# Mean squares of the attended tokens from small fp32 matmuls, and values of the key stage on other partitions

## The chip, the cores and the metric

One core of a Trainium2 chip runs the whole program. The metric is the device time of one execution in microseconds (us); the median of three runs stands for the kernel.

## The reference

Attention through a small set of packed tokens, followed by two feed-forward blocks. With 8 batches, 8 heads, 576 tokens of 64 numbers a head and 32 packed tokens a head:

```python
p_packed = sm_attn(p, k, v)                  # 32 packed tokens a head look at the keys
out = sm_attn(q, p_packed, p_packed)         # 576 tokens a head look at the 32 packed ones
x = out.transpose(0, 2, 1, 3).reshape(4608, 512)
xn = x / sqrt(mean(x * x, axis=-1) + 1e-06) * rms_g
x = (silu(xn @ w_gate) * (xn @ w_val)) @ w_out      # 512 -> 1536 -> 512
h = x @ w2_in                                        # 512 -> 2048
return (h * cos(h)) @ w2_out                         # 2048 -> 512
```

`sm_attn` is softmax attention with the maximum subtracted. All results are fp32; the weights arrive as 64-bit floats.

## The kernel before, in words

The program goes through three stages.

The **key stage** works on 16 groups, each four heads of a batch, in a loop of 18 rounds that handles several groups at different steps (lines 613 to 663). For a group it transposes the keys (`kp`), multiplies them with the packed tokens (`s`), takes the exponential (`e`), transposes it in 96-column chunks (`et`, copied to `eT`) and multiplies it with the values (`pp`, from the tile `vn`). The values of a group lie on 96 partitions, three blocks `m` of 32, each loaded by a DMA of its own (`load_v`, lines 345 to 352). The result `cd`, 32 packed outputs of four heads by 64 numbers, is stored to DRAM (`c`) and read again later. Beside this the loop narrows weights from 64 to 32 bits (`wy`, `ny`) and attends for batch 0.

The **projection stage** (lines 844 to 902) makes 24 iterations for each batch: in each, `gv_block` does 12 matmuls of 288 columns into two PSUM banks (gate and value), ScalarE and VectorE turn them into `silu` and `shl`, and `acc_block` does 6 matmuls of 512 columns of an earlier iteration into `acc`. Between them the attention of the next batch, `attend(b + 1)`, is fed in: it is a generator, and `att_step` advances it at two points of every iteration, by as many steps as its plan is due. All results of attention steps go through the pool of four banks that gate and value use (`ps_gv`); in the key stage, batch 0 uses a pool of two (`ps_bg`). `unit` makes a projection weight for a batch with 64x32 matmuls (`mps`).

The **last stage** does the second feed-forward block (`hp`, `ops`) and takes about half of the span.

In `attend`, softmax is done with 96 tokens on the partitions (tile `s`), in two halves `hf` of 288 tokens. The attended token itself is never formed: the weight `unit` makes is already multiplied with the packed outputs. Only its mean square is needed, so that `s` can be scaled by its inverse root. The steps are named in a string, two characters of which are the half and a part:

```python
    ATT_ORD = "t00 t01 x00 x01 x02 x03 t10 r00 t11 s00 x10 x11 p00 x12 p01 x13 - r10 - s10 - p10 p11"
```

Step `t` transposes the softmax of four heads into 128 rows (`atp`) and splits it into a high and a low part (`ahl`). Step `x` multiplies it with a block-diagonal matrix of packed outputs (`bdf`, split into `bdh`) by three matmuls (high by high, high by low, low by high: `mm3`), which gives two heads' 128 columns, squares the result on ScalarE and adds it into `ssq` on VectorE. Step `r` sums over the partitions with a matmul against ones (`rp`) and raises to the power -0.5 on GpSimd; `s` scales the softmax, `p` transposes it again for the projections (`apt`). A dash is a step that does nothing. The list for batch 0 is `ATT_ORD0`; its first `ATT_U` steps are done in the key stage's loop, the rest just behind it.

All instructions up to the middle of the last stage stand on each engine in the order in which the code issues them (`tc.manual_schedule()`); every DMA is issued by SyncE's queue.

Of the kernel before, what the change touches and what calls it, by code (L numbers as in the profile page):

```python
# [20 lines left out]
def kernel(  # L21
# [40 lines left out]
    REST = S - 512  # L62
    R_LOAD, R_SPLIT, S_AT = (1, 2), (4, 5), (20, 21, 24 + 1, 24 + 2)
# [3 lines left out]
    ATT_U, U_ATT = 34, 5  # L67
# [94 lines left out]
    nc.gpsimd.memset(ones, 1.0)  # L162
# [27 lines left out]
    bdf = a1.tile([128, 2, 4, D], F32, name="bdf")  # L190
    mhalf = a1.tile([CP, CH], F32, name="mhalf")
    for t in (bq, bdf):
        nc.gpsimd.memset(t, 0.0)
# [17 lines left out]
    def att_load(b):  # L211
        for r in range(2):
            rows = slice(r * 64, (r + 1) * 64)
            nc.sync.dma_start(out=bq[rows, :, r * NP:(r + 1) * NP], in_=q_dram[b][rows])
        for h in range(4):
            rows = slice(h * NP, (h + 1) * NP)
            nc.sync.dma_start(out=bdf[rows, :, h, :], in_=c_dram[b][rows])

    def attend(b):
# [28 lines left out]
        bdh = a1.tile([128, 2, 2, 4 * D], F32R, tag="bdh", name="bdh")  # L248
        hilo(bdf.rearrange("p g h d -> p g (h d)"), bdh[:, 0], bdh[:, 1])
# [18 lines left out]
        def transposed(dst, hf, kt):  # L268
# [6 lines left out]
            hilo(tp, dst[:, 0, kt], dst[:, 1, kt])  # L275

        z = [{}, {}]
# [6 lines left out]
        def a_x(hf, j):  # L284
            ahl = z[hf]["ahl"]
            if j == 0:
                z[hf]["acc"] = a1.tile([128, HALF], F32, tag="ssq", name="ssq")
            acc = z[hf]["acc"]
            g, r = divmod(j, 2)
            xp = psb[0].tile([128, HALF], F32, tag="mm", name="xp")  # L290
            mm3(
                xp, bdh[:, 0, g, r * 128:(r + 1) * 128], bdh[:, 1, g, r * 128:(r + 1) * 128],
                ahl[:, 0, g], ahl[:, 1, g], True, True,
            )
            if j == 0:
                nc.scalar.activation(out=acc, in_=xp, func=AF.Square)
            else:
                sq = a1.tile([128, HALF], F32, tag="sq", name="sq")
                nc.scalar.activation(out=sq, in_=xp, func=AF.Square)
                nc.vector.tensor_tensor(out=acc, in0=acc, in1=sq, op=ALU.add)  # L300

        def a_r(hf, _):
            acc = z[hf]["acc"]
            rp = psb[0].tile([CP, CH], F32, tag="mm", name="rp")
            for c in range(CH):
                nc.tensor.matmul(rp[:, c:c + 1], acc[:, c * CP:(c + 1) * CP], ones[:, 0:1], start=True, stop=True)
            ri = z[hf]["ri"] = a2.tile([CP, 2, CH], F32, tag="ri", name="ri")
            nc.vector.tensor_scalar(
                out=ri[:, 0], in0=rp, scalar1=1.0 / DM, scalar2=1e-6, op0=ALU.mult, op1=ALU.add
# [3 lines left out]
        def a_s(hf, _):  # L313
            ri = z[hf]["ri"]
            for c in range(CH):
                cc = hf * CH + c
                nc.vector.tensor_scalar(
                    out=s[:, cc], in0=s[:, cc], scalar1=ri[:, 1, c:c + 1], scalar2=None, op0=ALU.mult
                )

        def a_p(hf, kt):
            if kt == 0:
                ap_t[b, hf] = a3p[0].tile([128, 2, 2, HALF], F32R, tag="apt", name="apt")
            transposed(ap_t[b, hf], hf, kt)
# [288 lines left out]
    for i in range(NG + 2):  # L613
# [10 lines left out]
        if i == U_ATT:  # L624
            att_load(0)
# [420 lines left out]
```

## Time and profile before

| | |
|---|---|
| median of 3 runs (lowest to highest) | 1711.57 us (1710.38 to 1719.77) |
| profiled execution | 1720.5 us, of which the span of its instructions is 1718.7 |
| TensorE matmuls busy | 1657.4 us, 96% of the span |
| TensorE weight loads busy | 1378.2 us, 80% |
| VectorE (DVE) busy | 1009.4 us, 59% |
| ScalarE (ACT) busy | 848.7 us, 49% |
| GpSimd (POOL) busy | 78.3 us, 5% |
| mean granted clock of TensorE | 0.984 |

PE is TensorE's matmuls, PEld its weight loads, SP SyncE. Matmuls are pipelined: one begins before the one before it has ended, so the cost of a matmul in a dense stretch is the distance from its start to the next start, not its duration. An fp32 matmul of the program appears as two matmuls in the trace, one of fp32r (the split parts) as one; a transpose is one. A wait is put down to the instruction that came last by the profile; where the one named had long been done, it was another, often a DMA.

### The profile page before, as it was taken

Reading aid. Unit: us, or ns where it says so; the run is one execution under the profiler, and the core shown is the slowest. Engines: PE = TensorE matmul, PEld = TensorE weight load, DVE = VectorE, ACT = ScalarE, POOL = GpSimd, SP = SyncE. Lnnn points to the kernel's source line nnn. Section 1 sums busy time; section 2 is a strip of 40 time slices with the busy share of each in tenths; the row PEclk is TensorE's granted clock in tenths of the full one; section 3 lists DMA queues with packets and bytes.
Section 4 is the critical chain, followed back from the end, with each engine's and each line's share of the span. In section 5 each row is a group of like instructions: output and inputs, shape, how many; then the busy total and the mean of one; then the engine's idle time right before and its main releaser. Section 6 shows DMA issues by size and latency. Waiting matters only on the chain.

```text
span 1718.7 us, 26344 instructions
## 1 busy us (share of the span) xinstructions
PE 1657.4 (96%) x10176; PEld 1378.2 (80%) x10176; DVE 1009.4 (59%) x1958; ACT 848.7 (49%) x1595; POOL 78.3 (5%) x81
## 2 busy tenths in 40 slices
PE   6777989999999999999999999999999999999998
PEld 4555778888888888888888888888888888888887
DVE  2567875656565656665343675656555556565554
ACT  3454555545454545454433554545454545554453
POOL 0000431000000000000011000000000000000000
PEclk9887999999999999999999999999999999999999
DMA  9996745454545545543246010100000000000001
GB/s 203 247 284 172 223 147 162 138 171 142 177 128 167 154 139 163 166 139 108 77 135 256 25 54 21 34 16 28 22 25 25 25 25 25 25 0 25 1 25 25
DMA packets 112285, 177.36 MB, mean 103 GB/s; under 512 B 50208, under 2 KB 64544, under 8 KB 112160
## 3 DMA queue, kind: packets, MB, share of 16 engines
q1 hardware_dynamic: 112160, 175.68, 34.6%
q8 instruction: 80, 1.31, 0.3%
q14 instruction: 45, 0.37, 0.1%
HBM read 134.22 MB, written 41.42 MB: 102 GB/s over the span
## 4 chain that ended last, share of the span: by engine, by line
PE 84%; DMA 0%; DVE 0%; SPq 0%; issue 0%
PE hp L159 8%; PE hp L157 8%; PE hp L158 8%; PE ops L159 8%; PE ops L157 8%; PE ops L158 8%; PE gv L157 6%; PE acc L157 5%; PE gv L158 5%; PE gv L159 5%; PE acc L159 5%; PE acc L158 5%; PE mps L558 2%; PE sp L237 1%; PE atp L271 1%; PE qtp L227 1%
## 5 line engine op out<-in xcount | busy, mean ns | idle before, releaser
L157 PE MATMUL gv<-apt,wmhl 128*128 128x288 f32 x768 | 236.9, 308 | 2.4 <-DVE ahl L106 1.4
L158 PE MATMUL gv<-apt,wmhl 128*128 128x288 f32 x768 | 227.0, 296 | 0.0
L159 PE MATMUL gv<-apt,wmhl 128*128 128x288 f32 x768 | 226.7, 295 | 0.0
L158 PE MATMUL hp<-xhl,wmhl 128*128 128x512 f32 x576 | 224.1, 389 | 0.0
L159 PE MATMUL hp<-xhl,wmhl 128*128 128x512 f32 x576 | 224.1, 389 | 0.0
L157 PE MATMUL ops<-w2hl,ghl 128*128 128x512 f32 x576 | 224.1, 389 | 0.0
L158 PE MATMUL ops<-w2hl,ghl 128*128 128x512 f32 x576 | 224.1, 389 | 0.0
L157 PE MATMUL hp<-xhl,wmhl 128*128 128x512 f32 x576 | 223.9, 389 | 0.0
L159 PE MATMUL ops<-w2hl,ghl 128*128 128x512 f32 x576 | 222.3, 389 | 0.0
L946 ACT ACTIVATE r<-r 128x512 f32<-128x512 f32 x144 | 91.0, 632 | 250.0 <-DVE r L945 250.0
L954 DVE TENSOR_TENSOR r<-r,hp 128x512 f32<-128x512 f32 x144 | 98.8, 686 | 164.8 <-ACT r L947 164.7
L157 PEld LDWEIGHTS gv<-apt,wmhl 128*128 128x128 f32 x768 | 144.9, 189 | 44.5 <-issue 10.2
L157 PE MATMUL acc<-shl,wohl 128*128 128x512 f32 x432 | 175.8, 407 | 0.4 <-DMA shl<-s 0.4
L158 PE MATMUL acc<-shl,wohl 128*128 128x512 f32 x432 | 169.9, 393 | 2.8 <-DVE shl L753 2.8
L159 PE MATMUL acc<-shl,wohl 128*128 128x512 f32 x432 | 170.4, 394 | 0.0
L941 ACT ACTIVATE kk<-hp,magic 128x512 f32<-128x512 f32 x144 | 99.1, 688 | 117.4 <-PE hp L159 117.2
L742 DVE TENSOR_TENSOR silu<-silu,gv 128x288 f32<-128x288 f32 x192 | 86.5, 450 | 113.3 <-PE gv L159 96.7
L749 ACT ACTIVATE shl<-silu 128x288 fp32r<-128x288 f32 x192 | 85.1, 443 | 132.4 <-DVE silu L742 131.4
L158 PEld LDWEIGHTS gv<-apt,wmhl 128*128 128x128 f32 x768 | 145.1, 189 | 3.2
L159 PEld LDWEIGHTS gv<-apt,wmhl 128*128 128x128 f32 x768 | 144.6, 188 | 0.0
L942 DVE TENSOR_SCALAR kk<-kk 128x512 f32<-128x512 f32 x144 | 61.4, 426 | 116.2 <-ACT kk L941 116.1
L159 PEld LDWEIGHTS hp<-xhl,wmhl 128*128 128x128 f32 x576 | 108.2, 188 | 22.6
(126 smaller groups left out, 2857.6 us busy)
## 6 DMA issues: line engine op xcount, KB each, us to landing
wy<-wy SPq DMA_DIRECT2D x96, 512.0 KB, 4.4
kn<-in_k_dram SPq DMA_DIRECT2D x16, 576.0 KB, 7.7
vn<-in_v_dram SPq DMA_DIRECT2D x48, 192.0 KB, 6.6
qnat<-in_q_dram SPq DMA_DIRECT2D x32, 288.0 KB, 4.8
x_dram<-x SPq DMA_DIRECT2D x18, 512.0 KB, 3.2
x1raw<-x_dram SPq DMA_DIRECT2D x18, 512.0 KB, 4.0
raw<-in_moe_w_in_dram SPq DMA_DIRECT2D x16, 512.0 KB, 4.3
raw<-in_moe_w_out_dram SPq DMA_DIRECT2D x16, 512.0 KB, 4.2
```

The lines of the kernel that those rows point to most:

```text
L157: nc.tensor.matmul(ps, lhi, rhi, start=first, stop=False)
L158: nc.tensor.matmul(ps, lhi, rlo, start=False, stop=False)
L159: nc.tensor.matmul(ps, llo, rhi, start=False, stop=last)
L227: nc.tensor.transpose(tp[:, c * CP:(c + 1) * CP], qv[:, i, 2 * c:2 * c + 2, :].rearrange("p c d -> p (c d)"), ident[:CP, :CP],)
L237: nc.tensor.matmul(sp[:, i, 2 * c:2 * c + 2, :], qT[:, i, c * CP:(c + 1) * CP], bq[:, 2 * j + i], start=True, stop=True,)
L558: nc.tensor.matmul(ps[kt][h * NP:(h + 1) * NP], ppT[b // 4][rows, 4 * kt + h, n:n + NP], w_y[2 * u + kt][rows, j], start=True, stop=True,)
L742: nc.vector.tensor_tensor(out=t, in0=t, in1=pss[1], op=ALU.mult)
L749: nc.scalar.activation(out=sh[:, 0, cols], in_=t, func=AF.Copy)
L941: nc.scalar.activation(out=kk, in_=hp, func=AF.Identity, scale=1.0 / TWO_PI, bias=magic[:, 0:1])
L942: nc.vector.tensor_scalar(out=kk, in0=kk, scalar1=-MAGIC, scalar2=None, op0=ALU.add)
L946: nc.scalar.activation(out=r, in_=r, func=AF.Abs)
L954: nc.vector.tensor_tensor(out=r, in0=r, in1=hp, op=ALU.mult)
```

## The change

The mean squares are computed with unsplit fp32 operands, a head at a time. Step `t` only copies the transposed softmax (`at`, all four pieces of a batch in one tile). The packed outputs are loaded as they are stored (`cl`, one DMA a batch at its own place), not into a block-diagonal tile, and aren't split. Step `x` now takes a group `kt` of four heads: for each half and head one matmul of 32 rows (the head's packed tokens) and 64 columns (its numbers), the first half to PSUM partitions 0 to 63, the second to 64 to 127, each head in a bank of its own. So the four banks hold all tokens of the four heads. They are squared and summed as before, and one `r` step does both halves: `ones` has a column for the upper and one for the lower 64 partitions. There are two `x` steps a batch (for batch 0, whose pool has two banks, two heads at a time). An `x` step beside the projections runs between the two halves of an `acc_block` (the argument `mid`); the attention's plan has 38 steps in place of 45, and the key stage's loop does 29 steps of batch 0 in place of 34.

In the key stage, values lie on partitions 16 to 111 of a 128-partition tile whose other rows are zero; the blocks are loaded in the order 0, 2, 1. The exponential gets 16 zero columns at either end, and is transposed in pieces of 128 columns that begin 16 ahead of each chunk, so that rows and values meet. Three fixed value tiles take the place of a rotating buffer of three, and `cd` has two buffers in place of three.

```diff
+    V_P = 16
-    ATT_U, U_ATT = 34, 5
+    ATT_U, U_ATT = 29, 5
...
-    ATT_ORD = "t00 t01 x00 x01 x02 x03 t10 r00 t11 s00 x10 x11 p00 x12 p01 x13 - r10 - s10 - p10 p11"
-    ATT_ORD0 = "t00 t01 x00 x01 x02 x03 r00 s00 t10 t11 x10 x11 x12 x13 r10 s10 p00 p01 p10 p11"
-    AL_AT = 16
-    ATT_FROM, ATT_TO, ATT_FROM0, N_ATT = 0, 48, 10, 45
+    ATT_ORD = "t00 t10 - x00 t01 t11 - x10 - - r00 - s00 p00 p01 s10 p10 p11"
+    ATT_ORD0 = "t00 t10 x00 x01 t01 t11 x10 x11 - r00 - s00 s10 p00 p01 p10 p11"
+    AL_AT, CL_AT = 16, 21
+    ATT_FROM, ATT_TO, ATT_FROM0, N_ATT = 0, 48, 10, 38
...
-    nc.gpsimd.memset(ones, 1.0)
+    nc.gpsimd.memset(ones, 0.0)
+    for r in range(2):
+        nc.gpsimd.memset(ones[r * 64:(r + 1) * 64, r:r + 1], 1.0)
...
-        for h in range(4):
-            rows = slice(h * NP, (h + 1) * NP)
-            nc.sync.dma_start(out=bdf[rows, :, h, :], in_=c_dram[b][rows])
+
+    def att_load_c(b):
+        nc.sync.dma_start(out=cl, in_=c_dram[b])
...
-        bdh = a1.tile([128, 2, 2, 4 * D], F32R, tag="bdh", name="bdh")
-        hilo(bdf.rearrange("p g h d -> p g (h d)"), bdh[:, 0], bdh[:, 1])
...
         def a_t(hf, kt):
-            if kt == 0:
-                z[hf]["ahl"] = a1.tile([128, 2, 2, HALF], F32R, tag="ahl", name="ahl")
-            transposed(z[hf]["ahl"], hf, kt)
+            if (hf, kt) == (0, 0):
+                z["at"] = a1.tile([128, 2, 2, HALF], F32, tag="at", name="at")
+            nc.scalar.activation(out=z["at"][:, kt, hf], in_=transposed(hf, kt), func=AF.Copy)
...
+        def a_x(kt, part):
+            at = z["at"]
+            hs = range(4) if b else range(2 * part, 2 * part + 2)
+            xp = {h: psb[0].tile([128, HALF], F32, tag="mm", name="xp") for h in hs}
+            for hf in range(2):
+                for h in hs:
+                    rows = slice(h * NP, (h + 1) * NP)
+                    nc.tensor.matmul(
+                        xp[h][hf * 64:(hf + 1) * 64], cl[rows, kt, :], at[rows, kt, hf], start=True, stop=True
+                    )
+            for h in hs:
+                if (kt, h) == (0, 0):
+                    z["acc"] = a1.tile([128, HALF], F32, tag="ssq", name="ssq")
+                    nc.scalar.activation(out=z["acc"], in_=xp[h], func=AF.Square)
+                else:
+                    sq = a2.tile([128, HALF], F32, tag="sq", name="sq")
+                    nc.scalar.activation(out=sq, in_=xp[h], func=AF.Square)
+                    nc.vector.tensor_tensor(out=z["acc"], in0=z["acc"], in1=sq, op=ALU.add)
...
+    v_t = [u2.tile([128, 4, NC_, D], F32, tag=f"vn{x}", name="vn", bufs=1) for x in range(3)]
+    for x in range(2):
+        nc.vector.memset(v_t[x], 0.0)
+    e_pad = u2.tile([128, 2 * V_P + S], F32, tag="e", name="e", bufs=1)
+    for x in (slice(0, V_P), slice(V_P + S, 2 * V_P + S)):
+        nc.vector.memset(e_pad[:, x], 0.0)
...
-        for m in range(CH):
-            nc.sync.dma_start(out=vn[m * 32:(m + 1) * 32], in_=vs[m])
+        for m in (0, 2, 1):
+            nc.sync.dma_start(out=vn[V_P + m * 32:V_P + (m + 1) * 32], in_=vs[m])
...
-                nc.tensor.transpose(et[:, c, :], e[:, cc * CP:(cc + 1) * CP], ident)
+                nc.tensor.transpose(et[:, c, :], e_pad[:, cc * CP:cc * CP + 128], ident)
...
-    def acc_block(n, f, d2):
+    def acc_block(n, f, d2, mid=None):
...
         for r in range(2):
+            if r and mid:
+                mid()
...
-        while att is not None and att_done[0] < want:
+        while att is not None and att_done[0] < want and mid == (att_next[0] == "x"):
             att_done[0] += 1
-            next(att, None)
+            att_next[0] = next(att, None) or ""
...
-            acc_block(*seq[i - LAG])
+            acc_block(*seq[i - LAG], mid=(lambda: att_step(2 * i + 1, True)) if i < len(seq) else None)
```

The first place in the order is TensorE in a late batch of the projection stage, while batch 2 attends: an `x` step that stands ahead of a unit (`mps`), in the kernel before. `xp` is what the squares are taken of, a bracket names the engines (or DMA semaphores) that a row waits for.

```order
L157 MATMUL acc<-shl,wohl 128x512
L158 MATMUL acc<-shl,wohl 128x512
L159 MATMUL acc<-shl,wohl 128x512
L157 MATMUL xp<-ahl,bdh 128x288 [waits DVE_49]
L158 MATMUL xp<-ahl,bdh 128x288
L159 MATMUL xp<-ahl,bdh 128x288
L558 MATMUL mps<-wy,ppT_173 32x512 [waits DMAHW6_49,Activation_49]
L558 MATMUL mps<-wy,ppT_173 32x512 [waits DMAHW7_49,DVE_49]
L558 MATMUL mps<-wy,ppT_173 32x512 x6
```

After the change the same engine has this there: the first half of an acc block has just ended.

```order
L291 MATMUL xp<-at,cl 64x288 [waits DMAHW4_49,Activation_49]
L291 MATMUL xp<-at,cl 64x288 [waits DVE_49]
L291 MATMUL xp<-at,cl 64x288 [waits Activation_49]
L291 MATMUL xp<-at,cl 64x288 [waits DVE_49]
L291 MATMUL xp<-at,cl 64x288 x4
L158 MATMUL acc<-shl,wohl 128x512
L159 MATMUL acc<-shl,wohl 128x512
L160 MATMUL acc<-shl,wohl 128x512
L271 MATMUL atp<-ident,s 128x96 [waits Activation_49]
L271 MATMUL atp<-ident,s 128x96 x2
L566 MATMUL mps<-wy,ppT_175 32x512 [waits DMAHW5_49,Activation_49]
L566 MATMUL mps<-wy,ppT_175 32x512 [waits DMAHW6_49,Activation_49]
```

The `x` step has gone from the end of the acc block into its middle, waits for four banks one after the other, and the unit's matmuls behind it wait for ScalarE.

The second place is TensorE at the end of the key stage, from the last group's transposed exponentials to the first gate matmul, in the kernel before.

```order
L424 MATMUL et<-ident,e 96x128 x6
L452 MATMUL tp<-ident,cd 128x128
L157 MATMUL xp<-ahl,bdh 128x288
L158 MATMUL xp<-ahl,bdh 128x288
L159 MATMUL xp<-ahl,bdh 128x288
L438 MATMUL pp<-vn,eT 32x64 x24
L306 MATMUL rp<-ones,ssq 96x1 x3
L452 MATMUL tp<-ident,cd 128x128
L271 MATMUL atp<-ident,s 128x96 x12
L157 MATMUL gv_2116<-apt,wmhl 128x288
```

After the change:

```order
L432 MATMUL et<-ident,e 128x128 x6
L460 MATMUL tp<-ident,cd 128x128
L446 MATMUL pp<-vn,eT 32x64 x24
L460 MATMUL tp<-ident,cd 128x128
L271 MATMUL atp<-ident,s 128x96 x12
L158 MATMUL gv_2066<-apt,wmhl 128x288
```

The `x` and `r` steps of batch 0 no longer stand among the last groups' matmuls; they have moved to earlier rounds of the loop.

## Rows read from the trace of the kernel before

**Rows 1.** The page's busy times: us, share of the span, instructions.

```profile
PE 1657.4 (96%) x10176; PEld 1378.2 (80%) x10176; DVE 1009.4 (59%) x1958; ACT 848.7 (49%) x1595; POOL 78.3 (5%) x81
```

**Rows 2.** Windows: stretch, length, busy us (instructions) by engine, clock, DMA share, GB/s.

```profile
0.00:50.00 50.00, 32.94 (x360) 23.64 (x361) 12.91 (x39) 17.76 (x42) 3.94 (x20) 0.90 0.97 201
50.00:100.00 50.00, 40.57 (x495) 29.98 (x495) 27.98 (x69) 24.80 (x60) 1.62 (x6) 0.86 0.99 262
100.00:166.70 66.70, 45.47 (x626) 31.24 (x623) 47.70 (x120) 34.14 (x82) 3.21 (x5) 0.79 0.84 230
166.70:300.00 133.30, 124.79 (x900) 104.13 (x899) 95.30 (x191) 69.78 (x152) 39.77 (x26) 0.99 0.57 174
300.00:850.00 550.00, 550.00 (x3929) 471.35 (x3928) 329.33 (x732) 275.57 (x583) 14.08 (x12) 1.00 0.46 145
```

**Rows 3.** Timeline, PE, 29 to 49 us: start, us, instruction [idle before, releaser].

```profile
32.56 0.70 PE L381 MATMUL kp<-ident,kn 128*128 128x128 f32 x3 [3.01 <-ACT eT L425]
...
35.87 1.51 PE L438 MATMUL pp<-vn,eT 96*32 96x64 f32 x48 [1.66 <-DVE pT L369]
...
45.07 0.55 PE L381 MATMUL kp<-ident,kn 128*128 128x128 f32 x3 [3.08 <-ACT eT L425]
...
48.37 0.87 PE L438 MATMUL pp<-vn,eT 96*32 96x64 f32 x24 [2.00 <-DVE pT L369]
```

**Rows 4.** Timeline, ACT, ahead of the third of these pauses' end.

```profile
43.98 0.66 ACT L132 ACTIVATE wy<-wo 128x512 f32<-128x512 f32 x1 [7.11 <-DMA wo<-in_moe_w_gate_dram]
```

**Rows 5.** Timeline, PE, the end of the key stage.

```profile
156.38 0.40 PE L157 MATMUL xp<-ahl,bdh 128*128 128x288 f32 x1 [2.08 <-ACT ssq L296]
...
161.84 0.67 PE L306 MATMUL rp<-ones,ssq 128*96 128x1 f32 x6 [2.82 <-DVE ssq L300]
...
164.81 2.18 PE L271 MATMUL atp<-ident,s 96*128 96x96 f32 x12 [2.12 <-DVE ppT L457]
166.69 0.59 PE L157 MATMUL gv<-apt,wmhl 128*128 128x288 f32 x1
```

**Rows 6.** Timeline, PE, a batch of the projection stage: an x and an r step.

```profile
320.78 0.29 PE L157 MATMUL xp<-ahl,bdh 128*128 128x288 f32 x1
...
321.18 0.40 PE L157 MATMUL acc<-shl,wohl 128*128 128x512 f32 x1
...
321.88 0.39 PE L157 MATMUL acc<-shl,wohl 128*128 128x512 f32 x1
...
326.24 0.59 PE L306 MATMUL rp<-ones,ssq 128*96 128x1 f32 x6
326.69 0.38 PE L157 MATMUL gv<-apt,wmhl 128*128 128x288 f32 x1
```

**Rows 7.** Timeline, PE, key stage: score matmuls in two forms, with the next start.

```profile
100.60 2.21 PE L396 MATMUL s<-kT,pT 64*128 64x288 f32 x16
102.74 0.33 PE L368 MATMUL pt<-ident,pn 128*128 128x128 f32 x1
...
109.12 0.72 PE L400 MATMUL s<-kT,pT 64*32 64x288 f32 x16
109.76 0.33 PE L368 MATMUL pt<-ident,pn 128*128 128x128 f32 x1
```

**Rows 8.** Timeline, 315 to 317 us: last gv matmul, multiply, Square, shl copy.

```profile
315.68 0.29 PE L159 MATMUL gv<-apt,wmhl 128*128 128x288 f32 x1
...
316.08 0.45 DVE L742 TENSOR_TENSOR silu<-silu,gv 128x288 f32<-128x288 f32 x1
...
316.40 0.41 ACT L296 ACTIVATE ssq<-xp 128x288 f32<-128x288 f32 x1 [0.72 <-PE xp L159]
316.71 0.44 ACT L749 ACTIVATE shl<-silu 128x288 fp32r<-128x288 f32 x1
```

**Rows 9.** Groups by form, DVE: busy us, mean ns of one, idle before.

```profile
L106 DVE TENSOR_TENSOR ahl<-atp,ahl 128x288 fp32r<-128x288 f32 x32 | 14.6, 457 | 11.6 <-ACT ahl L105 11.3
...
L106 DVE TENSOR_TENSOR bdh<-bdf,bdh 128x512 fp32r<-128x512 f32 x8 | 5.4, 678 | 0.0
```

More of the change, by code (lines that the diff above doesn't have):

```diff
@@ L189 @@
     bq = a1.tile([128, H, 2 * NP], F32, name="bq")
[L190 to L193, printed above, removed]
+    cl = a1.tile([128, 2, D], F32, name="cl")
+    mhalf = a1.tile([CP, 2 * CH], F32, name="mhalf")
+    nc.gpsimd.memset(bq, 0.0)
     nc.gpsimd.memset(mhalf, -0.5)
@@ L274, in transposed @@
                 )
-            hilo(tp, dst[:, 0, kt], dst[:, 1, kt])
-        z = [{}, {}]
+            return tp
+        z = {}
         def a_t(hf, kt):
-            if kt == 0:
-                z[hf]["ahl"] = a1.tile([128, 2, 2, HALF], F32R, tag="ahl", name="ahl")
-            transposed(z[hf]["ahl"], hf, kt)
[L284 to L300, printed above, removed]
@@ L305, in a_r @@
+        def a_r(*_):
+            acc = z["acc"]
+            rp = psb[0].tile([CP, CH, 2], F32, tag="mm", name="rp")
             for c in range(CH):
-                nc.tensor.matmul(rp[:, c:c + 1], acc[:, c * CP:(c + 1) * CP], ones[:, 0:1], start=True, stop=True)
-            ri = z[hf]["ri"] = a2.tile([CP, 2, CH], F32, tag="ri", name="ri")
+                nc.tensor.matmul(rp[:, c], acc[:, c * CP:(c + 1) * CP], ones, start=True, stop=True)
+            ri = z["ri"] = a2.tile([CP, 2, 2 * CH], F32, tag="ri", name="ri")
@@ L308, in a_r @@
             nc.vector.tensor_scalar(
-                out=ri[:, 0], in0=rp, scalar1=1.0 / DM, scalar2=1e-6, op0=ALU.mult, op1=ALU.add
+                out=ri[:, 0], in0=rp.rearrange("p c t -> p (c t)"), scalar1=1.0 / DM, scalar2=1e-6,
+                op0=ALU.mult, op1=ALU.add,
             )
@@ L317, in a_s @@
                 nc.vector.tensor_scalar(
-                    out=s[:, cc], in0=s[:, cc], scalar1=ri[:, 1, c:c + 1], scalar2=None, op0=ALU.mult
+                    out=s[:, cc], in0=s[:, cc], scalar1=ri[:, 1, 2 * c + hf:2 * c + hf + 1], scalar2=None, op0=ALU.mult
                 )
@@ L323, in a_p @@
                 ap_t[b, hf] = a3p[0].tile([128, 2, 2, HALF], F32R, tag="apt", name="apt")
-            transposed(ap_t[b, hf], hf, kt)
+            hilo(transposed(hf, kt), ap_t[b, hf][:, 0, kt], ap_t[b, hf][:, 1, kt])
         fs = {"t": a_t, "x": a_x, "r": a_r, "s": a_s, "p": a_p}
-        for word in (ATT_ORD if b else ATT_ORD0).split():
+        words = (ATT_ORD if b else ATT_ORD0).split()
+        for word, nxt in zip(words, words[1:] + [""]):
             if word != "-":
                 fs[word[0]](int(word[1]), int(word[2]))
-            yield
+            yield nxt[:1]
+    v_t = [u2.tile([128, 4, NC_, D], F32, tag=f"vn{x}", name="vn", bufs=1) for x in range(3)]
[4 more added lines that the diff above has]
+        nc.vector.memset(e_pad[:, x], 0.0)
     nat_k, nat_v = {}, {}
@@ L410, in u_e @@
         s1, mx = z["s1"], z["mx"]
-        e = z["e"] = u2.tile([128, 2, HALF], F32, tag="e", name="e", bufs=1)
+        e = e_pad[:, V_P:V_P + S].rearrange("p (a s) -> p a s", a=2)
         nc.scalar.activation(
@@ L440, in u_pp @@
                 )
-        cd = u2.tile([128, 2, D], F32, tag="cd", name="cd", bufs=3)
+        cd = u2.tile([128, 2, D], F32, tag="cd", name="cd", bufs=2)
         nc.vector.tensor_scalar(
@@ L610 @@
     u_kt(0, range(CH))
+    nc.gpsimd.memset(v_t[2], 0.0)
     w_q, wo_q = [], []
@@ L625 @@
             att_load(0)
+            att_load_c(0)
         if 0 < i <= NG:
@@ L794 @@
     att_load(1)
+    att_load_c(1)
     bx = {}
@@ L830, with att_step @@
     att = None
-    def att_step(pt):
+    att_next = [""]
+    def att_step(pt, mid=False):
         b, x = divmod(pt, 4 * NF1)
@@ L881 @@
             att_load(b + 2)
+        if j == CL_AT and b < B - 2:
+            att_load_c(b + 2)
         if b == B - 1:
```

14 lines of the change are left out of this document (5 added, 9 removed).

## The prediction

> **What bounds the kernel now.** I read the page's busy times first: TensorE's matmuls cover 96% of the span, so the other engines matter only where TensorE waits for them [rows 1]. The windows then divide the span [rows 2]. From 300 to 850 us, where batch after batch goes through gate, value and output projection while the next batch attends, TensorE is busy in every one of the 550 us at clock 1.00: an instruction taken out there shortens the span by its distance to the next start. From 166.7 to 300 us it is idle 8.5 us, beside a vector engine busy 95.3 of 133.3 us. The key stage before 166.7 us is another regime: TensorE is idle for 17 of the first 50 us while the DMA engines are busy for 0.97 of the time and move only 201 GB/s, against 262 GB/s at a busy share of 0.99 in the next 50 us.
>
> In the timeline of that stage four pauses between 29 and 49 us make 3.01 + 3.08 + 1.66 + 2.00 = 9.75 us [rows 3]. They are put down to ScalarE and VectorE, but ScalarE itself had sat 7.11 us in front of a weight tile's landing and ran the waited-for copies only behind it [rows 4]: a DMA wait handed down. At the end of the stage three pauses of 2.08 + 2.82 + 2.12 = 7.02 us belong to the last norm steps of batch 0, and the projections start only at 166.69 us [rows 5].
>
> **The matmuls of the mean squares (A).** Before, an x step is three matmuls of 288 columns; from its first start to the next work's start is 321.18 - 320.78 = 0.40 us, and a batch has eight: 3.2 us. The two r steps take 326.69 - 326.24 = 0.45 us each, together 0.9 [rows 6]. After, a batch has two x steps of eight fp32 matmuls (32 rows, 64 columns, 288 moving columns) and one r step of three matmuls in place of six, half of 0.45: 0.23 us. The trace has no 32-row matmul. Its nearest rows are two forms of the score matmul, eight fp32 matmuls of 288 columns in either (16 in the trace, since each fp32 matmul is two there) [rows 7]. In 64x32 tiles, of which the array holds eight, they take 109.76 - 109.12 = 0.64 us; in 64x128 tiles, of which two go beside each other, 102.74 - 100.60 = 2.14 us. The new form also makes eight distinct tiles (four row blocks by two column halves), so I stay by the first and add 0.1 us for entering and leaving the tiled form in the middle of the acc matmuls: 0.75 us. Per batch: 3.2 + 0.9 - 2 x 0.75 - 0.23 = 2.37 us; the seven batches that attend beside the projections give 16.6 us. Bounds: 18 us at 0.64, and -3 us at 2.14.
>
> **What four banks at once cost (B).** Before, an x step took one of the four banks. Now it takes all four; the gate and value results just made must have left theirs. In the sampled block the last gv matmul starts at 315.68 and the multiply that frees the value bank ends at 316.53 [rows 8]; half an acc block, 321.88 - 321.18 = 0.70 us [rows 6], covers all of that but about 0.1, more where a vector instruction stands ahead of the multiply: I take 0.25 us, twice a batch. Behind x00 the order list shows the other half of acc, three transposes and then a unit's mps matmuls, which need the second and third bank. Four Squares of 0.41 us follow each other on ScalarE [rows 8]: the third is done about 1.3 us after the x step, TensorE arrives after 0.70 + 0.2: 0.5 us. With 0.2 us for gate matmuls that come early it is 1.2 us a batch, -8.4 us in seven. Bounds: 0.5 us a batch; and 2.8 if each step stands until all four Squares (1.64) and one 0.44 us copy ahead of them [rows 8] are through, less the 0.70 that covers them, twice.
>
> **Less vector work (C).** Four ahl subtractions of 0.457 and the bdh one of 0.678 go, 2.5 us of DVE a batch [rows 9]. In the full stretch that is worth nothing; it is hidden behind TensorE. Batch 1 attends between 166.7 and 300 us, where TensorE loses 8.5 us to a full DVE: I take 1.5, bounds 0 and 2.5.
>
> **The end of the key stage (D).** The new list for batch 0 is nine words shorter up to its r step, so x and r stand in earlier iterations; the order list shows nothing of batch 0 between the last two groups' matmuls, and only twelve transposes behind them. The three pauses (7.02 us) lose their cause. In their place the r step stands directly behind a unit and waits for its evacuation as the transposes did before; and all six scalings of s come in one go on VectorE, ahead of the last transposes. I take 5 us; bounds 0 (weights and DVE then set the end) and 7.0.
>
> **The values' new place (E).** Loads, bytes and packets stay; three blocks of 32 partitions go to 16-47, 80-111 and 48-79 instead of 0-31, 32-63 and 64-95. The transposes and the pp matmuls keep their columns and grow only in rows; memsets of the padded tiles (VectorE for two, GpSimd for the third) run before the first values are issued, under the wait for the first keys; without that cover the first pp matmuls would come later by a memset, once. Four 16 KB loads per batch become one, off the path. No row tells a transfer's speed by partition. Bounds: nothing, and the 9.75 us of [rows 3]. I take 3, nearer to nothing, since a load is still one block of 32 partitions.
>
> **The sum.** 16.6 - 8.4 + 1.5 + 5 + 3 = 17.7 us. The profiled execution took 1720.5 us, its span 1718.7, so 1.8 us lie around the span; it stands 8.9 us above the median of 1711.57, a difference I can't place, so I subtract from both: 1702.8 for that execution, 1694 us for the median.
>
> **The rivals.** (1) *Row blocks take turns.* If the four 32-row blocks don't work beside each other, an x step is long. All eight in turn cost twice 2.14, 4.28 us: A becomes 7 x (4.1 - 0.23 - 8.56) = -33 us, and the kernel takes about 1711.6 + 33 + 8.4 - 9.5 = 1743 us. Two at a time (2.14): A is -3, sum -1.9, 1713. The kernel is unchanged at about 2 us a step and slower by 0.5% from 2.6 us. For it: no row with 32-row tiles. Against it: 0.64 us for eight tiles of another cut.
>
> (2) *Evacuation takes over.* With matmuls of 0.75 us in front of 1.64 us of Squares, B becomes 2.8 a batch, 19.6 us; the sum falls to 6.5, 1705 us. For it: ScalarE also carries silu, the shl copy and weight narrowing in order. Against it: those waits are covered by 0.70 us on either side, and ScalarE is busy 276 of 550 us there [rows 2]. [...]
>
> (3) *The key stage doesn't move.* If D and E are nothing because weight loads set the pace, the sum is 9.7: 1702 us. For it: a DMA share of 0.84 to the stage's end [rows 2].
>
> (4) *The new partitions free the loads.* Then E is the whole 9.75 and D 7.0: sum 26.5, 1685 us. For it: the low 201 GB/s at full busy share in just the stretch in which values and keys arrive most densely. [...]
>
> **Chances and range.** The forecast (about 1687 to 1701) 0.50; evacuation 0.17; key stage unmoved 0.13; freed loads 0.10; row blocks in pairs 0.05, all in turn 0.05. A measurement of this kernel can tell about 0.5%, 8.6 us: faster is below 1703.0, slower above 1720.1. Faster: the forecast, the freed loads and half of the unmoved key stage, 0.66. Slower: blocks in turn and some mishap of two cases at once, 0.08. Same: the rest, 0.26. The range reaches from the freed loads, a little past 1685, to two at a time, 1713: 1684 to 1714 us; the forecast's own is 1687 to 1701.
>
> **What would show it.** Right: an x step from its first start to the next acc matmul near 0.75 us; TensorE's idle before xp near 0.25 us; the first gv matmul near 158 us instead of 166.69; the gv stretch from there to the last batch shorter by 8 to 10 us; the same rate in the last 800 us. A distance above 1.5 us per x step says row blocks take turns; long waits of mps or gv for Square say evacuation; pauses at 29 to 49 us gone, at a higher rate of the DMA engines, says the partitions matter. What would make the prediction wrong: a wait for a landing that takes the place of those at the end of the key stage, or a stop in front of each x step that half an acc block doesn't cover.

## The result, and the profile after

| | before | after |
|---|---|---|
| median of 4 runs (lowest to highest), us | 1711.87 (1710.38 to 1719.77) | 1695.68 (1691.54 to 1697.83) |
| ratio to before, 95% interval | | 0.9897 (0.9874 to 0.9920) |
| profiled execution, and its span, us | 1720.5, 1718.7 | 1695.08, 1693.3 |
| first gate matmul, us | 166.69 | 157.63 |
| first to last gate or value matmul, us | 724.87 | 708.00 |
| from there to the end of the span, us | 827.14 | 827.67 |

The kernel became 1.0% faster, 1.7 us above the predicted 1694. The last three lines come from the start times of the `gv` matmuls in the timeline and divide the difference of the two spans, 25.4 us, into 9.06 us of key stage and 16.87 us of projections, less 0.53 behind them. The division is not the predicted one: there the projections had 9.7 us and the key stage 8. Since the execution of before that was profiled stood 8.9 us above the median of the three runs, the 9.06 can't be trusted yet; the experiments come back to that.

The page of the changed kernel, busy times (as [rows 1]):

```profile
PE 1642.1 (97%) x10192; PEld 1352.0 (80%) x10192; DVE 997.6 (59%) x1922; ACT 826.1 (49%) x1575; POOL 74.5 (4%) x75
```

The windows, cut at the new first gate matmul (as [rows 2]):

```profile
0.00:50.00 50.00, 38.04 (x395) 28.10 (x395) 19.37 (x53) 20.54 (x49) 5.21 (x23) 0.90 1.02 242
50.00:100.00 50.00, 41.06 (x557) 29.71 (x555) 31.09 (x76) 24.47 (x60) 1.43 (x6) 0.90 1.05 277
100.00:157.63 57.63, 38.50 (x529) 24.56 (x530) 39.04 (x99) 30.77 (x76) 1.92 (x3) 0.75 0.77 217
157.63:300.00 142.37, 136.42 (x981) 112.67 (x981) 103.00 (x206) 74.84 (x162) 40.05 (x25) 0.99 0.56 174
300.00:850.00 550.00, 550.00 (x4016) 462.71 (x4015) 320.37 (x704) 261.87 (x581) 15.27 (x10) 1.00 0.47 149
```

TensorE is again busy in every one of the 550 us, so a step's price is still a distance between starts. The timeline of TensorE around an `x` step of a middle batch (as [rows 6]) gives it:

```profile
312.53 0.40 PE L158 MATMUL acc<-shl,wohl 128*128 128x512 f32 x1
312.76 0.40 PE L159 MATMUL acc<-shl,wohl 128*128 128x512 f32 x1
313.00 0.40 PE L160 MATMUL acc<-shl,wohl 128*128 128x512 f32 x1
313.32 0.74 PE L291 MATMUL xp<-at,cl 32*64 32x288 f32 x16
313.99 0.50 PE L158 MATMUL acc<-shl,wohl 128*128 128x512 f32 x1
314.33 0.39 PE L159 MATMUL acc<-shl,wohl 128*128 128x512 f32 x1
314.56 0.39 PE L160 MATMUL acc<-shl,wohl 128*128 128x512 f32 x1
314.79 0.41 PE L271 MATMUL atp<-ident,s 96*128 96x96 f32 x3
315.13 1.14 PE L566 MATMUL mps<-wy,ppT 64*32 64x512 f32 x16
316.20 0.40 PE L158 MATMUL gv<-apt,wmhl 128*128 128x288 f32 x1
```

The eight fp32 matmuls take 313.99 - 313.32 = 0.67 us from start to start. No bracket stands in these rows: TensorE doesn't wait ahead of `x`, and not ahead of the unit either. What the step costs around itself stands where the tile shape changes: the `acc` matmul ahead of it has 0.32 us to the next start instead of 0.23 or 0.24, the one behind it 0.34. (The run below that puts the step at the end of the block has 0.32 us ahead of it too, where the multiply had ended at 318.75 us and the step starts at 319.51.) ScalarE and VectorE at the same place (as [rows 8]):

```profile
312.80 0.45 DVE L752 TENSOR_TENSOR silu<-silu,gv 128x288 f32<-128x288 f32 x1 [1.56 <-PE gv L160]
...
314.12 0.41 ACT L297 ACTIVATE ssq<-xp 128x288 f32<-128x288 f32 x1 [0.39 <-PE xp L291]
314.43 0.71 ACT L300 ACTIVATE sq<-xp 128x288 f32<-128x288 f32 x2
...
315.42 0.42 ACT L300 ACTIVATE sq<-xp 128x288 f32<-128x288 f32 x1 [0.28 <-DVE ssq L301]
```

The multiply that frees the value bank ends at 313.25, just ahead of 313.32. The third Square ends at 315.14, just where the unit starts, at 315.13. Both covers hold, with little to spare.

A steady batch, from the first gate matmul to that of the next batch, takes 434.84 - 345.25 = 89.59 us, where before it took 452.55 - 360.73 = 91.82, and 91.65 to 91.67 in the five others. Adding up start-to-start distances over such a batch: `x` 3.27 us before and 1.34 after, `r` 0.91 and 0.45, all else 0.31 more (the rows around `x`, and 0.15 at the transposes of q). So a batch wins 2.39 - 0.31 = 2.08 us. The 288 matmuls beside which batch 1 attends went from 102.39 to 98.02 us: those 2.08 and 2.29 more. Not all of the 2.29 belongs to the change in vector work. One transpose of q waited for its load there before (1.47 us in the second profile of before, below), and not in the changed kernel, where a gate matmul waits for a Square instead (the first row is of before, the second of after):

```profile
197.07 0.47 PE L227 MATMUL qtp<-ident,qnat 96*128 96x96 f32 x3 [1.48 <-DMA qnat<-in_q_dram]
```
```profile
235.20 0.40 PE L158 MATMUL gv<-apt,wmhl 128*128 128x288 f32 x1 [0.88 <-ACT sq L300]
```

At the end of the key stage (as [rows 5]) the last rows of TensorE's timeline read:

```profile
136.39 0.71 PE L291 MATMUL xp<-at,cl 32*64 32x288 f32 x8
137.03 0.88 PE L446 MATMUL pp<-vn,eT 128*32 128x64 f32 x48
140.80 2.26 PE L566 MATMUL mps<-wy,ppT 64*32 64x512 f32 x16 [2.89 <-ACT sq L300]
144.51 1.12 PE L307 MATMUL rp<-ones,ssq 128*96 128x2 f32 x6 [1.45 <-DVE wmhl L107]
...
146.94 1.21 PE L409 MATMUL s<-kT,pT 64*32 64x288 f32 x16
...
154.43 0.33 PE L460 MATMUL tp<-ident,cd 128*128 128x128 f32 x1 [1.87 <-DVE cd L450]
155.81 2.12 PE L271 MATMUL atp<-ident,s 96*128 96x96 f32 x12 [1.04 <-DVE s L319]
157.63 0.59 PE L158 MATMUL gv<-apt,wmhl 128*128 128x288 f32 x1
```

Behind the last score matmul (`s`), two of the three pauses of [rows 5] are gone, those of 2.08 and 2.82 us. The third, 2.12 us ahead of the last transposes, is not: 1.87 and 1.04 us stand there now. New pauses stand ahead of the last score matmul: a unit waits for the Squares, `r` for the unit's evacuation.

### The profile page after: what moved, and what is told of

It is laid out like the page before. It is cut to its first block, busy times and chain, and to the rows that moved or that the text cites. A ratio compares the mean times of both kernels' runs of the same rounds, so it can differ in the third digit from the quotient of the medians.

```text
span 1693.3 us, 26314 instructions
## 1 busy us (share of the span) xinstructions
PE 1642.1 (97%) x10192; PEld 1352.0 (80%) x10192; DVE 997.6 (59%) x1922; ACT 826.1 (49%) x1575; POOL 74.5 (4%) x75
## 4 chain that ended last, share of the span: by engine, by line
PE 85%; DMA 1%; DVE 0%; SPq 0%; issue 0%; ACT 0%; ACTq 0%
PE hp L160 8%; PE hp L159 8%; PE hp L158 8%; PE ops L160 8%; PE ops L159 8%; PE ops L158 8%; PE gv L158 6%; PE acc L158 6%; PE gv L159 5%; PE gv L160 5%; PE acc L160 5%; PE acc L159 5%; PE mps L566 2%; PE sp L239 1%; PE atp L271 1%; PE qtp L229 1%
## 5 line engine op out<-in xcount | busy, mean ns | idle before, releaser
L751 ACT ACTIVATE silu<-gv 128x288 f32<-128x288 f32 x192 | 78.8, 410 | 103.2 <-PE gv L160 102.9
```

The lines of the kernel that those rows point to most:

```text
L751: nc.scalar.activation(out=t, in_=pss[0], func=AF.Silu)
```

## The experiments

The runs of before that stood beside the experiments, 40 in all with those above, have a median of 1715.05 us (1709.24 to 1721.26); the 8 of the changed kernel, 1696.1 (1691.54 to 1698.07). These are 18.9 us apart. Ratios are each to the runs of before of the same sitting. A mark that the texts use: the start of the **12th** of the 16 score matmuls in the key stage (101.20 us in the changed kernel). Two of the texts call it the 13th group's by a miscount; the numbers given there are those of the 12th.

**The key stage once more.** Both kernels as they are, the changed one first:

> The changed kernel once more, beside the two others. Its first gate matmul shows how far the key stage varies from execution to execution: if what was seen is the rule, it stands within 1 us of 157.6 us, and the median within 2 us of 1695.7.

Measured: 1696.28 us median of 4, ratio 0.9885 (0.9862 to 0.9908). The first gate matmul came at 160.50 us, not within 1 us of 157.63. The kernel before, unaltered:

> The kernel before once more, for its profile. The profiled execution before lay 8.9 us above its median. If the key stage's length was its own, the first gate matmul stands at 166.7 us again; if that execution had a long key stage, it stands at 157 to 160 us, and the changed kernel's key stage is no shorter. The stretch of gate and value matmuls: 724.9 us again.

Measured: 1716.03 us; first gate matmul 162.48 us, stretch of gate and value matmuls 724.79. So the key stage of the first profile of before was 4.2 us longer than that of the second, and the changed kernel's varies as well. That the first profile after the change met the forecast of 158 us was one execution's luck. Two more executions of the same key stage come from runs below that change only the projections: 155.22 and 162.57 us. Windows of the first 50 us, in the order of the changed kernel's second execution, these two, and the second of before:

```profile
0.00:50.00 50.00, 35.57 (x377) 26.21 (x379) 16.52 (x46) 19.61 (x45) 5.21 (x23) 0.90 1.01 228
```
```profile
0.00:50.00 50.00, 38.86 (x451) 28.85 (x453) 19.50 (x53) 22.28 (x52) 5.22 (x23) 0.93 1.01 248
```
```profile
0.00:50.00 50.00, 35.08 (x375) 26.25 (x377) 15.38 (x42) 19.72 (x45) 5.23 (x23) 0.90 0.99 223
```
```profile
0.00:50.00 50.00, 36.34 (x374) 26.05 (x376) 15.47 (x44) 19.21 (x45) 4.19 (x21) 0.91 0.99 221
```

At a DMA share near 1.0 the same key stage moved 223 to 248 GB/s, and the higher the rate, the earlier the first gate matmul (248: 155.22; 242: 157.63; 228: 160.50; 223: 162.57). The 201 GB/s of [rows 2] was one execution's, and so was a part of the 9.75 us of pauses in [rows 3]: the second of before has 6.3 us there, in three pauses, and the four of the changed key stage have 3.6 to 7.7 us in pauses of over 1 us.

**Where the values lie.** Only the partitions undone:

```diff
-    V_P = 16
+    V_P = 0
-    e_pad = u2.tile([128, 2 * V_P + S], F32, tag="e", name="e", bufs=1)
+    e_pad = u2.tile([128, 32 + S], F32, tag="e", name="e", bufs=1)
-    for x in (slice(0, V_P), slice(V_P + S, 2 * V_P + S)):
+    for x in (slice(V_P + S, 32 + S),):
```

> The changed kernel with one thing undone: the values lie on partitions 0 to 95 again (the same fixed tiles, the same 128-row transposes, the same order of loads). Theory 'the partitions free the loads' (rival 4): the first 50 us move about 201 GB/s again where the changed kernel moved 242, the first gate matmul comes about 5 to 9 us later than 157.6, and the time is 1701 to 1705 us. Theory 'placement is nothing' (the first gate matmul came earlier because of the norm steps of batch 0, and because the profiled execution of the kernel before was a long one): first gate matmul within 1.5 us of 157.6, time 1694 to 1698 us.

Measured: 1694.87 us, ratio 0.9879 (0.9859 to 0.9900); first gate matmul 159.28 us; 222 GB/s in the first 50 us. Then the values' part undone wholly (`vn` of 96 partitions in rotating buffers, pieces of 96 columns, order 0, 1, 2):

```diff
-        vn = nat_v[i] = v_t[i % len(v_t)]
+        vn = nat_v[i] = u2.tile([CP, 4, NC_, D], F32, tag="vn", name="vn", bufs=3)
-        for m in (0, 2, 1):
-            nc.sync.dma_start(out=vn[V_P + m * 32:V_P + (m + 1) * 32], in_=vs[m])
+        for m in range(CH):
+            nc.sync.dma_start(out=vn[m * 32:(m + 1) * 32], in_=vs[m])
...
-                nc.tensor.transpose(et[:, c, :], e_pad[:, cc * CP:cc * CP + 128], ident)
+                nc.tensor.transpose(et[:, c, :], e[:, cc * CP:(cc + 1) * CP], ident)
```

> The changed kernel with the values' part undone wholly: 96 partitions, rotating tiles, 96-row transposes, order 0, 1, 2; the norm steps as changed. By the sum of the prediction (D 5 us, E 3): 3 us over the changed kernel, 1698 to 1699 us. If the partitions free the loads: 1701 to 1705 us. If neither the key stage's norm steps nor the place of the values matter, 1695 us. In all three the stretch of gate and value matmuls keeps its 708 us (724.9 before).

Measured: 1694.64 us, ratio 0.9888 (0.9864 to 0.9912), stretch 708.84 us. Both stand beside the changed kernel's 0.9885; the new place is worth nothing that these times can tell. The rates do stand in the order of the place: 201, 221, 222 and 212 GB/s in the first 50 us of the four traced executions with values on partitions 0 to 95 (two of before and these two), 223 to 269 in the ten with 16 to 111. In this sitting, though, the two kernels with the lower rates have the lower medians (1694.87 and 1694.64 us against 1696.28). So whether the place gives some GB/s stays open; a gain of 3 us would have to show in these medians, and doesn't.

**Where the x steps stand.** First directly behind the gate and value matmuls:

```diff
+            att_step(2 * i + 1, True)
         elif part:
...
-            acc_block(*seq[i - LAG], mid=(lambda: att_step(2 * i + 1, True)) if i < len(seq) else None)
+            acc_block(*seq[i - LAG])
```

> The x steps beside the projections stand directly behind the gate and value matmuls, ahead of the whole acc block; all else as changed. Theory 'half an acc block covers the evacuation of gate and value' (why the bank waits cost nothing in the changed kernel): the fourth head's bank is free only 0.72 us after the x step's place (in one sampled block the multiply ends at 313.25 us, the x step would start at 312.53), so each of 14 steps stands about 0.6 us, a steady batch takes 90.6 to 90.9 us instead of 89.58, and the kernel 7 to 9 us longer than the changed one. Rival 'four banks are always free': batch 89.6, the same time.

Measured: 1704.68 us, ratio 0.9933 (0.9910 to 0.9955); a steady batch 90.87 us, 1.28 more; the stretch 716.22 us, 8.2 more than the changed kernel's. Its timeline, TensorE and VectorE:

```profile
310.50 0.29 PE L160 MATMUL gv<-apt,wmhl 128*128 128x288 f32 x1
310.73 1.41 PE L291 MATMUL xp<-at,cl 32*64 32x288 f32 x16
310.90 0.45 DVE L752 TENSOR_TENSOR silu<-silu,gv 128x288 f32<-128x288 f32 x1 [1.55 <-PE gv L160]
...
311.41 0.22 PEld L291 LDWEIGHTS xp<-at,cl 32*64 32x64 f32 x10 [0.49 <-DVE silu L752]
...
312.06 0.50 PE L158 MATMUL acc<-shl,wohl 128*128 128x512 f32 x1
```

The step takes 312.06 - 310.73 = 1.33 us instead of 0.67: it stops in its middle until the multiply has ended at 310.90 + 0.45 = 311.35. The row of its matmuls has no bracket for that, but the row of its weight loads (PEld) has. Then at the end of the `acc` block:

```diff
+                att_step(2 * i + 1, True)
                 att_step(2 * i + 1)
...
-            acc_block(*seq[i - LAG], mid=(lambda: att_step(2 * i + 1, True)) if i < len(seq) else None)
+            acc_block(*seq[i - LAG])
```

> The x steps beside the projections stand at the end of the acc block, directly ahead of what needs the banks next (gate matmuls, transposes or a unit), as in the kernel before. Theory 'the other half of acc covers the first Square': the first Square ends about 0.55 us after the x step, and the next work waits for its bank: 0.5 us ahead of gate matmuls, up to 1 us where transposes and a unit follow; a steady batch takes 90.6 to 91.6 us instead of 89.58, and the kernel 7 to 13 us longer than the changed one. Rival 'Squares cost nothing wherever they stand': batch 89.6, the same time.

Measured: 1708.41 us, ratio 0.9957 (0.9942 to 0.9972); a steady batch 90.92 us, 1.33 more; the stretch 716.48 us. Of the 12 us over the changed kernel the stretch shows 8.5. In the profiled execution the rest lies in a later first gate matmul (162.57 us), in a stage that the edit doesn't touch; why all four runs are that long I can't say. TensorE's timeline now has the wait in a bracket:

```profile
319.51 0.74 PE L291 MATMUL xp<-at,cl 32*64 32x288 f32 x16
320.31 0.41 ACT L297 ACTIVATE ssq<-xp 128x288 f32<-128x288 f32 x1 [1.08 <-PE xp L291]
...
320.77 0.47 PE L271 MATMUL atp<-ident,s 96*128 96x96 f32 x3 [0.52 <-ACT ssq L297]
```

Here the multiply has long ended, and the next work waits for the first Square. So on either side half an `acc` block hides about 0.65 us a step (half of 1.28 and of 1.33), and in the middle both are hidden.

**Early or late norm steps of batch 0.** The second pair of `x` steps and `r` go back among the last groups' matmuls, in their new form:

```diff
-    ATT_U, U_ATT = 29, 5
+    ATT_U, U_ATT = 34, 5
-    ATT_ORD0 = "t00 t10 x00 x01 t01 t11 x10 x11 - r00 - s00 s10 p00 p01 p10 p11"
+    ATT_ORD0 = "t00 t10 x00 x01 t01 t11 - - - - - x10 x11 - r00 - s00 s10 p00 p01 p10 p11"
```

> Five dashes stand ahead of batch 0's second pair of x steps, and the key stage's loop does 34 steps again: x and r of batch 0 stand among the last groups' matmuls, as before, in their new form. Theory 'swap' (the earlier place only moves the same waits in front of the last score matmul): from the start of the 13th group's score matmul to the first gate matmul 56 to 58 us as in the changed kernel (56.4) and before (57.7), the last group's score matmul about 4 us earlier and the stretch behind it about 4 us longer; the same median within 2 us. Theory of the prediction (D: 5 us from the earlier place): that distance 60 to 62 us, median about 1700 us.

Measured: 1692.86 us, ratio 0.9864 (0.9846 to 0.9881). From the 12th score matmul to the first gate matmul it took 53.8 us, less than either theory had. Once more, in another sitting:

> The kernel with batch 0's second x steps and r late, once more, since its first profile was one execution. If the late place is 2.6 us shorter by itself: 53.5 to 54.2 us from the 12th of 16 score matmuls to the first gate matmul again, whatever the loads did before it, and a median of 1691.5 to 1694.5 us, 2 to 4 us under the changed kernel. If the first profile was an exception: 55.5 to 57 us and 1695 to 1697 us.

Measured: 1693.16 us, ratio 0.9878 (0.9854 to 0.9901), 157.33 - 103.77 = 53.6 us. The distance holds from execution to execution, also in the changed kernel (56.4, 56.4, 56.1, 56.4 in four) and before (57.6, 57.8), while the mark itself moves from 98.75 to 109.12 us. TensorE's timeline of the second late run, from the mark to the last score matmul and behind it:

```profile
103.77 0.72 PE L409 MATMUL s<-kT,pT 64*32 64x288 f32 x16
...
136.10 1.32 PE L566 MATMUL mps<-wy,ppT 64*32 64x512 f32 x16
...
139.14 0.72 PE L409 MATMUL s<-kT,pT 64*32 64x288 f32 x16
...
141.48 0.71 PE L291 MATMUL xp<-at,cl 32*64 32x288 f32 x8
146.72 1.53 PE L291 MATMUL xp<-at,cl 32*64 32x288 f32 x8 [4.53 <-ACT sq L300]
...
157.33 0.59 PE L158 MATMUL gv<-apt,wmhl 128*128 128x288 f32 x1
```

From the mark to the last score matmul it is 35.4 us, where the changed kernel takes 146.94 - 101.20 = 45.7; behind it 18.2 instead of 10.7. The unit (`mps`) no longer waits for Squares. What the earlier place saved behind the last score matmul it cost ahead of it, and 2.7 us more. TensorE's mean granted clock over the distance, a mix of its two levels (1.00 and 0.50 in the traces of before and after), was 0.81 and 0.80 in the late runs, and 0.75, 0.78, 0.77 and 0.75 in the four with the changed key stage. Among those four the distance doesn't follow the clock (56.4, 56.4, 56.1 and 56.4 us), but no run holds the clock fixed, so that it has a part in the 2.7 us isn't excluded.

**What holds the rounds at the end of the key stage.** ScalarE's copies and Squares for batch 0 stand behind the exponential, which waits for VectorE's maximum (17.2 us over the 16 groups of the changed kernel), and that stands behind weight narrowing. In the first try the narrowing follows the maximum in all rounds:

```diff
-        if i <= NG:
-            w_late()
         if i < NG:
             u_e(i)
+        if i <= NG:
+            w_late()
...
-        if i < NG:
-            w_late()
-            w_late = lambda: None
```

> In the key stage's loop VectorE's second part of weight narrowing (up to two tiles of four instructions, 2.2 us each) stands behind the maximum of the next scores instead of ahead of it; all else as changed. Theory 'ScalarE's copies and Squares of batch 0 are late because they stand behind the exponential, and that behind VectorE's narrowing': the exponential starts 2 to 3 us earlier in a round, the waits of x, mps and et for ScalarE shrink, and from the 13th group's score matmul to the first gate matmul it takes 48 to 53 us instead of 56.4; median 1689 to 1693 us. Rival 'weight loads or other work set the pace of a round': that distance within 1.5 us of 56.4, the same median.

Measured: 1696.44 us, ratio 0.9885 (0.9868 to 0.9902). The distance shrank to 52.2 us, the median not at all: the mark stood at 109.08 us. Here the mark deceives, for the edit moved it. TensorE's rows from the score matmul before it to the mark:

```profile
96.68 2.21 PE L405 MATMUL s<-kT,pT 64*128 64x288 f32 x16
...
102.45 1.07 PE L566 MATMUL mps<-wy,ppT 64*32 64x512 f32 x10
...
106.53 1.15 PE L566 MATMUL mps<-wy,ppT 64*32 64x512 f32 x6 [3.01 <-DVE wy L153]
...
109.08 1.21 PE L409 MATMUL s<-kT,pT 64*32 64x288 f32 x16
```

A unit that stands ahead of the mark waits for the very narrowing that was put off. From the 11th score matmul to the 12th it takes 109.08 - 96.68 = 12.4 us, where the changed kernel takes 101.20 - 93.28 = 7.9; from the 11th to the first gate matmul it is 64.6 us against 64.4. So the theory isn't borne out: the order moved the wait from one side of the mark to the other. Next the same only from round 11 on (the lines at the end of a round stay, under `if i < 11:`): alone, then with the late norm steps, then that with three buffers for `cd`:

> The changed kernel with only the narrowing behind the maximum from round 11 on. Theory 'loads were delayed in the early rounds': median 1691 to 1693.5 us (the changed kernel 1696, less the 4.2 us by which the stretch from the 12th score matmul was shorter with this order in all rounds). Rival 'the end of the stage is paid for elsewhere, whatever the early rounds do': 1695 to 1697 us.

> Two edits together: batch 0's second x steps and r late again (as in the run with late norm steps, 53.8 us from the 12th of 16 score matmuls to the first gate matmul, median 1692.9 us), and the weight narrowing behind the maximum, but only from the loop's round 11 on. Theory 'each shortens the end of the stage by itself, and the narrowing behind the maximum lost its 4 us in the early rounds, where late narrowing frees weight buffers later and so delays loads': that distance 49 to 52 us, the 12th score matmul at 99 to 106 us as usual, median 1688 to 1691 us. Rival 'the two take the same waits away': distance 52 to 54 us, median 1692 to 1694 us.

> The same with three buffers for cd, as before the change. In the changed kernel VectorE stood 11.8 us in three waits for the store of cd. Theory 'those waits lie under the DMA engines' full stretch and cost nothing': the same median within 1.5 us. Rival 'they hold back the first 100 us': the 12th score matmul 2 to 4 us earlier, the median as much lower.

Measured: alone 1696.22 us, ratio 0.9871 (0.9849 to 0.9892), distance 54.1; with late steps 1694.32, 0.9869 (0.9849 to 0.9889), 54.7; with three buffers 1692.23, 0.9860 (0.9837 to 0.9884), 54.7. The first two medians are those of the rivals (the second just above 1692 to 1694), though the five runs of the first reach from 1691.09 to 1696.99 us and cover the theory's range as well. Alone, from round 11 on, the order shortened the distance by 2.3 us in its one profiled execution, and by the same from the 11th score matmul. The edits don't add: beside the late steps, whose distance is 53.7, the order of the narrowing gains nothing. That late narrowing in the early rounds delays the loads, as the theory had it, doesn't show: in the run with that order in all rounds the 11th score matmul came at 96.68 us, within the 91.2 to 98.2 of the four executions of the changed key stage. The third buffer's run has a median 2.1 us lower and its mark 3.0 us earlier (96.18 against 99.21), as its rival has it, but the intervals overlap and the mark moves as far by itself: open. VectorE's 11.8 us of waits for the store of `cd` are gone with it, as the groups by line show, of the changed kernel and of this one:

```profile
L450 DVE TENSOR_SCALAR cd<-pp,mx 128x128 f32<-128x128 f32 x16 | 5.5, 342 | 19.9 <-DMA c<-cd 11.8 <-PE pp L446 4.3 <-PE et L432 2.9
```
```profile
L450 DVE TENSOR_SCALAR cd<-pp,mx 128x128 f32<-128x128 f32 x16 | 5.5, 341 | 6.4 <-PE pp L446 6.4
```

The prediction has no term for the two buffers. In the changed kernel TensorE itself pauses behind such a wait:

```profile
38.16 1.54 PE L390 MATMUL kp<-ident,kn 128*128 128x128 f32 x6 [3.24 <-DVE cd L450]
```

A pause of `kp` put down to `cd`, of 1.5 to 5.1 us, stands in the first 50 us of ten of the eleven traces with two buffers and of none of the three with three. Whether it adds to the time, or lies under the loads that this stretch waits for anyway, these runs don't show.

## Why the prediction was right, and where it was not

The total was right, 17.7 us against 18.9, by sizes that erred in both directions. That they made up for each other is luck: the projections gave 16.8 us and not 9.7, the key stage about 2.8 and not 8.

**A, the matmuls: right.** Predicted 2.37 us a batch, measured 2.39 from start-to-start distances, by two small errors. An `x` step takes 0.67 us and not 0.75, since the 0.1 for entering and leaving the tiled form, an estimate that no row gave, falls on the `acc` matmuls around it (0.09 and 0.10 us by the rows above, counted under B). An `r` step stays at 0.45 us: "half of 0.45" was a misreading, as its row has six matmuls before and after. Rival 1 falls: 0.67 us for eight tiles of 32 rows, against 0.64 for the form of [rows 7] that the sum was tied to and 2.14 for the other. In the trace of before the first matmuls of the eight 64x32 tiles start within 0.05 us (109.12 to 109.16), those of the 64x128 form two at a time, from the second pair to the last 0.24 us from pair to pair. In the changed kernel the eight 32-row tiles start within 0.05 us as well (313.32 to 313.37).

**B, four banks at once: the term that was most mis-sized.** Predicted 1.2 us a batch, 8.4 in seven; measured 0.31 a batch, with the longer distances where the tile shape changes, about 2.2 in seven. The first 0.25 us was set for a vector instruction ahead of the multiply; none stands there in the batch shown, and no wait. The 0.5 us ahead of the unit is zero, since three transposes stand between and the third Square ends as the unit comes. The wait is real: the two runs that take the cover away pay 1.28 and 1.33 us a batch, just the predicted size, which I charged to a place where it is hidden. Rival 2 describes these two runs; in the steady batches of the changed kernel evacuation takes no time from TensorE beyond these 0.31 us, and beside batch 1's attention one gate matmul waits 0.88 us for a Square.

**C, less vector work: right in size, its reason not shown by itself.** 1.5 predicted, 2.29 us measured beside batch 1's attention, within its bounds of 0 and 2.5; TensorE's waits there fell from 8.0 to 5.7 us. But the prediction put the waits down to a full VectorE, and 1.5 of the 8.0 were the wait for the load of q. That wait is back, with 1.02 us, in the run with the values' part undone, and its batch 1 takes 98.90 us instead of 98.02. What is left without it is about 1 us, an estimate from these two runs: VectorE's gain, less the new wait of 0.88 us for a Square. No run undoes the vector work alone.

**D, the end of the key stage: wrong in its reason.** The step that failed is "the three pauses lose their cause". Two of them did; the third, ahead of the last transposes, went from 2.12 to 1.87 + 1.04 us. And the same `x` and `r` steps, put into earlier rounds, made a unit (2.89 us) and `r` (1.45 us) wait, and with them the last score matmul. From the mark the distance fell from 57.7 to 56.4 us, 1.3 us instead of 5, and with the steps in the old place it falls to 53.7. Against before, the late runs gain 4.0 us with the new form in the old place, of which the earlier place takes 2.7 back. (Counted from the 11th score matmul the numbers are 1.9, 4.6 and 2.7. The values' new place isn't taken out of the 4.0; undone by itself it leaves a distance of 56.9.)

**E, the values' place: nothing that the times show, instead of 3.** With values on partitions 0 to 95 the kernel is as fast: 1694.87 and 1694.64 us against 1696.28. The 9.75 us of [rows 3] were in part one execution's, and pauses there vary in the changed key stage too, from 3.6 to 7.7 us. Rival 4 falls with it. No run shows a transfer's speed by partition: the 3 us were my choice between two bounds, a gain in time from the place doesn't show here, and 223 to 248 GB/s come with one and the same placement.

Summed by what was measured: A and B 7 x 2.08 = 14.6, C 2.3, the stretch 16.8 as read. The span behind it is 0.7 us longer (827.7 in two executions against 827.0), which may be chance, since in the other runs, whose last stage is the same, it lies between 826.9 and 828.0. The medians of 40 and 8 runs, 18.9 us apart, leave 18.9 - 16.8 + 0.7 = 2.8 us for the key stage: 1.3 from the mark on, and 1.5 ahead of it that can't be told from the spread. Rival 3, the key stage that doesn't move, was nearer to the truth on its part than the forecast, and the projections made up for it.

The late norm steps beat the changed kernel by about 3 us: 1692.86 us as the median of the 10 runs of two sittings, against 1696.1 of 8. That is 0.2%, not measured side by side; the repeated distance of 53.7 against 56.4 us is the firmer ground. The run with three buffers had the lowest median, 1692.23, and isn't to be told from it.

## What to carry to other kernels

This stage, whose first 100 us had a DMA share of 0.97 to 1.05 in the first profiles of before and after, differed from execution to execution (first gate matmul at 155.2 to 162.6 us in four executions of the changed key stage): take the pauses of such a stage from two profiles or more, and measure edits inside it from a mark behind the last load that holds it up. Take a second mark as well: an edit can move the mark, as the one with the narrowing behind the maximum did. A step that needs many PSUM banks, as the `x` step here, belongs in the middle of other matmuls that use none of them: half the cover ahead for the results to leave, half behind for its own; at either end it cost 1.28 and 1.33 us a batch, what one side no longer hid. Moving a step to an earlier place isn't free because a pause at its old place goes (here the earlier place took back 2.7 of 4.0 us): look at which engines must evacuate it at the new one.

## What the runs showed of the hardware

- Eight fp32 matmuls of 32 rows, 64 columns and 288 moving columns, spread over four row blocks and two column halves, take 0.67 us from start to start, and the `acc` matmuls on either side of them, where the shape changes from and to 128 rows, have about 0.1 us more to the next start.
- The same key stage ran to its end in 155.2 to 162.6 us in four executions, with 223 to 248 GB/s in its first 50 us at a DMA share of 0.99 to 1.02; behind that, each of the two kernels repeated itself within 0.3 us in its two profiled executions.
- A wait in the middle of a group of matmuls can go without a bracket: the stopped `x` step's matmul row shows only 1.33 us from start to start, with TensorE counted as busy. The row of its weight loads shows the wait, with 0.49 us.
